# Convolution groups side by side: new places for the stages of entering chunks in rounds two and three

## The chip, the cores and the metric

The kernel runs on one core of one Trainium2 chip. The metric is the device time of one launch in microseconds (us), lower is better. Engines are named as the profile names them: PE (TensorE matmul), PEld (TensorE weight load), DVE (VectorE), ACT (ScalarE), POOL (GpSimd) and SP (SyncE, which only issues DMAs here).

## The reference

Eight batches of 4224 tokens with 192 channels pass through a causal convolution and then through a mixing block. Biases and norms are absent; this is all of it:

```python
w = softmax(weight, axis=-1)            # 8 heads x 7 taps
x = causal_conv(x, w)                   # 7 taps per head of 24 channels
theta = x @ w_theta                     # (192, 192)
zr, zi = x * cos(theta), x * sin(theta)
y = w_tok_r @ zr + w_tok_i @ zi         # two (4224, 4224) token matrices
u = x + y
out = u + maximum(u @ w_ch, 0.0)        # (192, 192)
```

The two token matrices carry nearly all of the arithmetic.

## The kernel before

**Tiles.** The 4224 tokens are cut into 33 input chunks of 128 tokens (`NK`) and 33 output blocks of 128 rows (`NT`). A chunk's tile `z` holds seven half-width products of `x`, cosine and sine (`Z11`, `T1`, `Z21`, `Z22`, `T2`, `T4`, `T3`). A fast matrix product with seven instead of eight block products works on *pairs* of output blocks. So one **step** (class `Step`) takes one pair of output blocks and all active chunks, and consists of seven **runs** (`runs`), one for each block product: for each active chunk two matmuls 128x384 at L443 (the "y" matmuls). Where only one output block is left the step has four runs. Between the runs a result is added into the SBUF tile `pv` by DVE (`give`, L408). The PSUM pool of the accumulators (`ypool`) has two buffers. Three accumulators `c1`, `c2` and `c3` use them in one step; `c3` opens in run six, in the buffer that `c2` left after run four, and the next step's `c1` opens in the buffer that `c3` left.

**Rounds.** At most eleven chunks are active (`NW`). There are 58 steps, numbered t = 0 to 57 here, and three rounds of chunks: 0 to 10, 11 to 21 and 22 to 32. A chunk stays for 17 steps (`NU`). `start` tells at which step it becomes active. Chunks of rounds two and three become active at steps 18 to 23 and 36 to 41, two at a time, but one alone (15 and 26) at steps 20 and 38. They are prepared one step earlier, in steps 17 to 22 and 35 to 40, between the y matmuls of the nine chunks that are active there (ten in steps 19 and 37). Step 40 has only four runs. The first round is prepared by a loop of its own at the end of the kernel.

**The stages of a chunk** (class `Chunk`, `tasks`) are nine: `conv(0)`, `conv(1)`, `transpose`, `theta(0)`, `theta(1)`, the two `product`s and the two `sums`. `conv(j)` is a *convolution group*: eight small matmuls 96x192 on 64 columns at L210 into a PSUM tile `pc`, which ACT copies into `z` (L151); after `conv(1)` SP writes the convolved rows to `xs` in DRAM (L227, four DMAs). `transpose` is twelve PE transposes (L165) and an ACT copy to `uT` (L151). `theta(g)` is eight matmuls (L141) and two ACT sines into `z` (L246). `product` (L251) and `sums` (L257) are DVE work. The PSUM tiles of `conv`, `transpose` and `theta` share one pool of two buffers (`mmpool`).

**Order.** The orders of PE, DVE and ACT are written out by hand: `in_order` ties each instruction to the one before it on its engine. `mix` yields the y matmuls, and at its places calls *events*: pairs of a place and a function, sorted by place. A place runs from 0 to 7 over the whole step, whatever its number of runs, and an event comes ahead of the first chunk whose place is not smaller than its own:

```python
while events and events[0][0] * len(runs) <= 7 * (r + c / self.n):
    events.pop(0)[1]()
```

`step_events(t)` gathers the events of step t: the weight work of step t+1 (`w_tasks`: `turn` at L336 turns a staged weight tile, `wsum` at L348 makes sums of them), the loads of the `pv` tiles of step t+1 at place 1.6 (`load_rows`, L372), the loads of the token matrices of step t+2 at 1.3 and 4.3 (`load_w`, L323, into two `st` buffers), the loads of the chunks that are prepared in step t+1 at 4.5 (`load_chunk`: four DMAs of `x` from POOL at L197, and at L188 four of the 16 rows of history from the chunk before, from SP), and the nine stages of each chunk that becomes active at t+1. SP writes finished `pv` tiles to `part` at the end of a step (L456). SP's own queue and the `x` loads are not tied by hand; the framework places them.

Of the kernel before, what the change touches and what calls it, by code (L numbers as in the profile page):

```python
# [16 lines left out]
def kernel(  # L17
# [34 lines left out]
    NK = S // P  # L52
# [8 lines left out]
    NW = 11  # L61
# [4 lines left out]
    start = [base[k % NW] + (NU + 1) * (k // NW) for k in range(NK)]  # L66
# [20 lines left out]
    def dve(ins):  # L87
        return in_order("dve", ins)
# [4 lines left out]
    def pool(ins):  # L93
        return in_order("pool", ins)
# [31 lines left out]
    def channel_pieces(w):  # L126

        return ((slice(0, P), 0, w[0:P, :]), (slice(0, R), 1, w[P:D, :]),
                (slice(R, P), 2, w[0:R, :]), (slice(0, P), 3, w[R:D, :]))
# [145 lines left out]
    def load_chunk(k):  # L275
        if k < NK and k not in chunks:
            chunks[k] = Chunk(k, before=chunks[k - 1] if k % NW else None)
# [235 lines left out]
    def step_events(t):  # L513
        found = []
        s = steps[t]
        if t + 1 < NSTEP:
            found += steps[t + 1].w_tasks()
            found.append((1.6, steps[t + 1].load_rows))
            for i in steps[t + 1].adds:
                found.append((2 + 2 * i, lambda i=i: steps[t + 1].load_x(i)))  # L520
                found.append((3.6 + 2 * i, lambda i=i: steps[t + 1].add_x(i)))
        here = [(r, i, which) for r in steps for i, when, which in r.ahead if when == t]
        for j, (r, i, which) in enumerate(here):
            found.append((1.5 + 1.8 * j, lambda r=r, i=i, which=which: r.add_ahead(i, which)))
        if t + 2 < NSTEP:
            nxt = steps[t + 2]
            for m in (1, 2):
                found.append((1.3 + 3 * (m - 1), lambda m=m: nxt.load_w(m)))
        if t == NU - 2:
            def load_wch():  # L530
                dve(nc.vector.memset(wch[:, 1:3, :], 0.0))
                for rows, i, part_w in channel_pieces(moe_w_ch):
                    pool(nc.gpsimd.dma_start(out=wch[rows, i, :], in_=part_w))
            found.append((3, load_wch))
        for at, f in outputs:
            begin = at - sum(s.time for s in steps[:t])
            if 0 <= begin < steps[t].time:
                found.append((7 * begin / steps[t].time, f))
        if t >= NU - 2:
            new = [k for k in range(NK) if start[k] == t + 2 and k >= NW]  # L540
            for k in new:
                found.append((4.5, lambda k=k: load_chunk(k)))
            at = 0.1
            for k in (k for k in range(NK) if start[k] == t + 1 and k >= NW):
                pos = [0, .5, 1.4, 2.2, 2.6, 3.1, 3.15, 3.4, 3.6]

                def add(at, j, k):
                    def go():
                        if j == 0:
                            chunks[k].todo = chunks[k].tasks()  # L550
                        next(chunks[k].todo)()
                    found.append((at, go))
                for j, p in enumerate(pos):
                    add(at + p, j, k)
                at += 2.3
        return found


# [62 lines left out]
    for q in range(Q):  # L621
# [3 lines left out]
            start=True, stop=True,  # L625
# [11 lines left out]
    def stream():  # L637
        for t in range(NSTEP):
            yield from steps[t].mix(step_events(t))
# [104 lines left out]
```

## Time and profile before

| | us |
|---|---|
| three runs | 1448.31, 1449.44, 1449.76 |
| median | 1449.44 |
| span of the profiled execution, its own time | 1444.6 |
| PE busy | 1414.5 (98%) |
| DVE busy | 978.2 (68%) |
| POOL busy, ACT busy | 434.6 (30%), 316.2 (22%) |

The span runs from the first to the last instruction of the one execution that was profiled. Nothing around it is recorded for that execution; the three runs lie 3.7 to 5.2 us above it. The mean granted TensorE clock was 0.997. "Busy" of PE is the union of matmuls whose ends are modelled, so it does not say how fast they follow each other. The window 380 to 580 holds the entering steps of round two, 840 to 1030 those of round three.

### The profile page before, as it was taken

The page shows a single profiled execution, that of the slowest core. Times are in us where ns is not written, and L with a number is a line of the kernel's source. Part 1 is how long each engine was busy: PE and PEld are TensorE (multiplying, and loading weights), DVE is VectorE, ACT ScalarE, POOL GpSimd, SP SyncE. Part 2 cuts the span into 40 slices and gives each one's busy share as a digit, 9 for nine tenths or more (in the row PEclk, how much of TensorE's full clock was granted, in tenths as well). Part 3 has the DMA queues.
Part 4 walks back from the last instruction along what each step waited for, and adds up shares of the span by engine and source line. Part 5 has one row for each costly group of instructions (what it writes and reads, how often), then busy time and mean ns, then how long its engine had stood idle before and what let it go on. Part 6 is the DMA issues. An engine that isn't in the chain of part 4 may idle for free.

```text
span 1444.6 us, 23749 instructions
## 1 busy us (share of the span) xinstructions
PE 1414.5 (98%) x9809; PEld 886.3 (61%) x9809; DVE 978.2 (68%) x1050; ACT 316.2 (22%) x379; POOL 434.6 (30%) x655
## 2 busy tenths in 40 slices
PE   7899999999999999999999999999999999999997
PEld 4656666666666666666666666666666666666665
DVE  6893554555448687866666657876877677767686
ACT  6851101111124254000000004435210110010133
POOL 8421211111223232432433343233323123213120
PEclk9999999999999999999999999999999999999999
DMA  9975756564699999897899889989999999898883
GB/s 181 253 148 136 146 119 133 98 152 87 152 229 210 226 244 222 219 265 173 223 245 222 233 155 239 235 181 237 274 220 202 213 204 221 204 200 193 166 232 116
DMA packets 272029, 281.99 MB, mean 195 GB/s; under 512 B 106672, under 2 KB 240176, under 8 KB 271920
## 3 DMA queue, kind: packets, MB, share of 16 engines
q0 software_dynamic: 162464, 92.15, 48.4%
q1 hardware_dynamic: 71824, 178.88, 35.2%
q10 hardware_dynamic: 37632, 9.44, 4.3%
q8 instruction: 77, 1.26, 0.4%
q14 instruction: 32, 0.26, 0.1%
HBM read 245.49 MB, written 108.13 MB: 245 GB/s over the span
## 4 chain that ended last, share of the span: by engine, by line
PE 89%; DVE 3%; DMA 2%; ACT 2%; POOL 1%; issue 1%; SPq 0%; DVEq 0%; ACTq 0%; POOLq 0%
PE y L443 81%; PE v L141 5%; PE pc L210 1%; PE tp L165 1%; ACT z L246 1%; DVE pv L408 1%; DMA xw<-xw 1%; POOL xw L197 1%; DMA xw<-in_x_dram 1%; DVE z L257 1%; POOL st L323 1%; DVE z L251 1%; DMA pv<-part 1%; ACT uT L151 1%; DVE wt L336 0%
## 5 line engine op out<-in xcount | busy, mean ns | idle before, releaser
L443 PE MATMUL y<-z,wt 128*128 128x384 f16 x7656 | 1283.6, 326 | 10.4 <-DVE pv L408 7.3
L443 PEld LDWEIGHTS <-wt 128*128 128x128 f16 x7656 | 740.7, 98 | 488.1 <-issue 10.2
L408 DVE TENSOR_TENSOR pv<-y,pv 128x768 f32<-128x768 f32 x324 | 309.2, 955 | 327.0 <-PE y L443 286.8
L336 DVE STREAM_TRANSPOSE wt<-st 128x1408 f16<-128x1408 f16 (+7 forms) x224 | 327.8, 1465 | 45.8 <-PE y L443 39.1
L323 POOL DMA_DIRECT2D st<-in_moe_w_tok_r_dram x232 | 132.4, 579 | 464.9 <-DVE wt L336 459.4
L323 POOL DMA_DIRECT2D st<-in_moe_w_tok_i_dram x232 | 132.5, 580 | 405.4 <-DVE wt L336 397.5
L348 DVE TENSOR_TENSOR wt<-wt 128x1408 f16<-128x1408 f16 (+7 forms) x216 | 176.1, 815 | 40.5 <-PE y L443 38.0
L151 ACT ACTIVATE z<-pc 128x768 f16<-128x768 f32 x65 | 53.3, 820 | 386.7 <-PE pc L210 386.5
L151 ACT ACTIVATE ub<-pv 128x768 f16<-128x768 f32 x63 | 50.2, 835 | 333.2 <-DVE pv L408 310.7
L406 ACT ACTIVATE pv<-y 128x768 f32<-128x768 f32 x66 | 54.0, 819 | 281.6 <-PE y L443 281.6
L141 PEld LDWEIGHTS <-uT 128*128 128x128 f16 x1056 | 91.1, 98 | 27.4 <-issue 8.5
L386 POOL TENSOR_TENSOR pv<-pv,xr 128x1536 f32<-128x1536 f32 x24 | 74.5, 3105 | 67.1 <-DVE pv L476 21.9
L197 POOL DMA_DIRECT2D xw<-in_x_dram x132 | 76.5, 591 | 30.1 <-DMA xw<-xw 9.7
L476 DVE SCALAR_TENSOR_TENSOR pv<-v,pv 128x768 f32<-128x768 f32 x66 | 62.9, 954 | 27.5 <-PE v L141 27.0
L151 ACT ACTIVATE uT<-tp 128x1536 f16<-128x1536 f16 (+1 forms) x49 | 59.7, 1221 | 74.4 <-PE tp L165 74.4
L257 DVE TENSOR_TENSOR z<-z 128x768 f16<-128x768 f16 x132 | 73.4, 556 | 3.6
L246 ACT ACTIVATE z<-v,half_pi 128x768 f16<-128x768 f32 x66 | 59.9, 907 | 42.1 <-PE v L141 41.7
L251 DVE TENSOR_TENSOR z<-z 128x1536 f16<-128x1536 f16 x66 | 60.1, 948 | 6.6 <-ACT z L246 6.6
L141 PE MATMUL v<-wth,uT 128*128 128x192 f16 x528 | 55.0, 248 | 5.6 <-ACT z L246 3.3
L141 PE MATMUL v<-wch,uT 128*128 128x192 f16 x528 | 54.2, 246 | 2.1 <-DVE pv L476 1.2
L246 ACT ACTIVATE z<-v 128x768 f16<-128x768 f32 x66 | 53.5, 810 | 0.0
L210 PE MATMUL pc<-xw,bands 96*64 96x192 f16 x528 | 35.3, 256 | 1.2 <-DVE bands L628 0.8
(43 smaller groups left out, 138.0 us busy)
## 6 DMA issues: line engine op xcount, KB each, us to landing
part<-pv SPq DMA_DIRECT2D x79, 768.0 KB, 4.6
pv<-part SPq DMA_DIRECT2D x79, 768.0 KB, 6.0
out_dram<-pv SPq DMA_DIRECT2D x66, 384.0 KB, 4.3
st<-in_moe_w_tok_r_dram POOLq DMA_DIRECT2D x136, 176.0 KB, 5.7
st<-in_moe_w_tok_i_dram POOLq DMA_DIRECT2D x136, 176.0 KB, 5.1
xs<-z SPq DMA_DIRECT2D x132, 96.0 KB, 4.1
xw<-in_x_dram POOLq DMA_DIRECT2D x121, 96.0 KB, 5.9
xr<-xs SPq DMA_DIRECT2D x24, 384.0 KB, 4.5
```

The source lines that it names most:

```text
L141: pe(nc.tensor.matmul(v[:, k, b * D : (b + 1) * D], lhsT=tT[:, 3 * k + b + i, :], rhs=w[:, 2 * b + i, :], start=(i == 0), stop=(i == 1),))
L151: act(nc.scalar.activation(out=out, in_=in_, func=AT.Copy))
L197: nc.gpsimd.dma_start(out=self.xw[lo : lo + n, h, :, :], in_=x[:, t0 : t0 + n, :].rearrange("b s d -> s b d"),)
L246: act(nc.scalar.activation(**args))
L251: dve(nc.vector.tensor_tensor(out=o, in0=xv, in1=o, op=ALU.mult))
L257: dve(nc.vector.tensor_tensor(out=z[:, o, :], in0=z[:, a, :], in1=z[:, b, :], op=ALU.subtract))
L323: pool(nc.gpsimd.dma_start(out=st[a * Q : (a + 1) * Q, 0:nb, :, 0:n] .rearrange("i r bt s -> i (r bt) s"), in_=w[self.tbs[0] * P : (self.t ...
L336: dve(nc.vector.transpose(self.w[name][:, 0 : self.n, :, :], self.st[int(name[1])][:, int(name[0]) - 1, :, 0 : self.n * Q] .rearrange("p b ...
L348: dve(nc.vector.tensor_tensor(out=self.w[name][:, 0 : self.n, :, :], in0=self.w[a][:, 0 : self.n, :, :], in1=self.w[b][:, 0 : self.n, :, : ...
L386: ins = pool(nc.gpsimd.tensor_tensor(out=self.pv[i], in0=self.pv[i], in1=self.xr[i], op=ALU.add))
L408: dve(nc.vector.tensor_tensor(out=o, in0=yv, in1=o, op=ALU.add))
L443: pe(nc.tensor.matmul(y[cn][:, q, 0:BH], lhsT=self.w[wn][:, c, :, :].rearrange("p bt i -> p (bt i)"), rhs=chunks[k].z[:, zn, q * BH : (q + ...
```

## The change

Before, the second chunk of a step simply followed 2.3 places behind the first, with `conv(0)` and `conv(1)` half a place apart and the first chunk's stages at 0.1 plus the list `pos`. Now each of the two chunks has its own list of places, and both convolution groups of a chunk have the same place.

```diff
-            at = 0.1
-            for k in (k for k in range(NK) if start[k] == t + 1 and k >= NW):
-                pos = [0, .5, 1.4, 2.2, 2.6, 3.1, 3.15, 3.4, 3.6]
+            places = (
+                (.1, .1, 1.1, 2.75, 3.05, 3.6, 3.65, 3.9, 4.1),
+                (2.1, 2.1, 3.55, 4.6, 5.0, 5.5, 5.55, 5.8, 6.0),
+            )
+            new = [k for k in range(NK) if start[k] == t + 1 and k >= NW]
+            for k, pos in zip(new, places):
...
                 for j, p in enumerate(pos):
-                    add(at + p, j, k)
-                at += 2.3
+                    add(p, j, k)
```

The order of the nine numbers is that of the nine stages. In absolute places the list of the first chunk was 0.1, 0.6, 1.5, 2.3, 2.7, 3.2, 3.25, 3.5, 3.7, and that of the second chunk 2.4, 2.9, 3.8, 4.6, 5.0, 5.5, 5.55, 5.8, 6.0. No instruction is added or taken away.

## The prediction

> **What bounds the kernel now.** I read the page's busy times first (PE 98%), then the chain that ended last in order of time, since a busy PE does not say that it is fast.
>
> ```profile
> 102.48 315.10 PE y L443 x1938
> ...
> 571.62 295.75 PE y L443 x1820
> ```
>
> Outside the entering steps the chain is nothing but y matmuls: 315.10 / 1938 = 0.1626 us each. Steps without entering chunks can neither gain nor lose. Inside the entering steps I read PE's timeline, and, at the kernel's start, the one place where two convolution groups already stand together:
>
> ```profile
> 417.51 0.52 PE L210 MATMUL pc<-xw,bands 96*64 96x192 f16 x8
> 417.96 1.80 PE L443 MATMUL y<-z,wt 128*128 128x384 f16 x10
> 419.69 0.52 PE L210 MATMUL pc<-xw,bands 96*64 96x192 f16 x8
> ```
>
> ```profile
> 8.89 1.49 PE L210 MATMUL pc<-xw,bands 96*64 96x192 f16 x16 [0.78 <-DVE bands L628]
> ```
>
> From one group's start to the next, 419.69 - 417.51 = 2.18 us pass with ten y matmuls between (1.63): a lone group costs 0.55 us. Within a group the matmuls run in pairs (two halves of 64 columns). Sixteen in a row at the start last 1.49 us at about half clock; without the last matmul's 0.37 that is 1.12 over seven intervals, 0.16 a pair, so 0.08 at full clock, and no hole where the second group begins. Four pairs are 0.32 to 0.35 us. So going from y to convolution and back costs 0.20 to 0.23 us that a group standing behind another does not pay.
>
> Then the waits of PE: in the windows 380 to 580 and 840 to 1030 there are few, so stalls are no large pot. The longest is in the two steps with ten chunks, at 490.76 and 940.56; the chain around the first:
>
> ```profile
> 483.57 0.96 DVE pv L408
> 484.53 0.67 DVE wt L348
> 485.19 1.74 DVE z L251 x2
> 486.93 0.67 DVE wt L348
> 487.60 0.48 DVE z L257
> ...
> 489.84 0.88 DVE pv L408
> 490.72 0.04 issue
> 490.76 1.30 PE y L443 x7
> ```
>
> DVE gives run three, then S1, both products, S2 and all four sums, and only then the result of run four. `c3` waits for that buffer at the start of run six.
>
> **The change part by part.** Twelve steps (17 to 22, 35 to 40) prepare 22 chunks. The order of the built program confirms that all 22 have sixteen convolution matmuls in a row.
>
> *Adjacent groups.* I take 0.22 us a chunk (ends 0.20 and 0.23; bounded below by nothing, if the second group had to wait for its PSUM buffer: it uses the other of the two, long free, and the row at 8.89 shows no hole). Twenty chunks outside step 40: -4.4 us. [...]
>
> *Ten-chunk steps (19, 37).* S2 now stands ahead of the products and two of the four sums behind run four's give. From give three's start, by the rows of the chain: 0.9 + 0.67 + 0.67 + 1.74 + two sums 1.1 = 5.1, then the give 0.9: 6.0 us, where it was 7.2; and give three starts about 0.9 earlier (one theta of 0.66 and 0.22 no longer ahead of it). PE needs the buffer at run six, twenty chunk slots of 0.325 plus a theta behind run three's end, 7.2 us. The 0.73 us wait goes; with its ramp the y matmuls lose 0.9 each time. -1.8 us.
>
> *Nine-chunk steps, DVE.* At 429.73 to 445.3 DVE runs without idle time: it is nearly a second bound. Between gives three and six the same instructions lie (13.6 us by their starts, 429.73 to 443.37). Give three comes 0.65 us earlier, but products wait for theta(1)'s sine (ready 2.0 after give three's start; DVE gets there at 2.2, so no loss), and give four waits 0.3 for run four's end. So DVE ends 0.3 earlier while PE arrives 0.44 earlier; the next step's `c1` had 0.4 us to spare and keeps about 0.25. Where the weights of the next step are for ten chunks (steps 18 and 36; turns 1.50 for 1.37) that is overdrawn by about 0.15 each: +0.3 us, between 0 and 1.
>
> *ACT and PSUM buffers.* Two copies of 0.81 now follow each other; the second is done some 2.5 us into the step, the transposes come at 4.1. Transposes to theta: 18 or 20 y matmuls (2.9 us) cover the copy of 1.45. The sines of theta(0) (1.7) are over before the second transposes (2.9 after theta's end). Nothing is late; without this cover each chunk would lose up to 1.5.
>
> *Step 40.* Four runs, so places are dense. DVE is full to the last give at 1023.05 to 1024.0, which PE awaits at 1024.06. Before its products it stood idle 1.32 us for a sine; now S2 (0.88) fills that, while the sine comes about 0.15 later. PE resumes 0.7 earlier: -0.7, its two chunks' 0.44 included; theta(0)'s wait for `uT` remains (0.3 to 0.6) but is hidden behind this give.
>
> *SP and POOL.* The `xs` writes and the histories of the next chunks are issued 1 to 4 us earlier. In steps 17, 20, 35, 38 and 39 the first `pv` load stood ahead of the first `xs` writes, and now both `pv` loads stand behind them (some 3 us later for the first). They are needed a step later, so nothing waits, but they then move beside the `x` loads.
>
> *The second chunk's data.* This is the cost. Its first group comes 22 - 19 = 3 slots (0.97), a theta (0.66) and 0.22 earlier: 1.85 us, at 7.7 us into the step instead of 9.55. Its `x` is the last load that POOL issues in the step before, behind the token matrix, which waits for DVE's turn, and it shares the DMA engines with `part` (768 KB twice). Asked for the L197 loads at 890 to 893 and 441 to 444:
>
> ```profile
> L197 POOL DMA_DIRECT2D xw<-in_x_dram x4: 586/598/603, 890.5 to 892.2; - x4
> ...
> DMA to landing us min/median/max: 6.0/7.2/10.8
> ```
>
> ```profile
> L197 POOL DMA_DIRECT2D xw<-in_x_dram x4: 581/583/583, 441.9 to 443.6; - x4
> ...
> DMA to landing us min/median/max: 3.6/5.7/5.9
> ```
>
> Chunk 25's last load lands at 892.2 + 10.8 = 903.0, and its convolution starts at 903.26: 0.2 us to spare. Chunk 19's lands at 522.6 + 9.8 = 532.4 for 533.63: 1.2 to spare. Chunk 14's has 4.1, chunk 30's 5.9, the others more. POOL's issue keeps its distance to the step's end. With 1.85 less to spare, PE waits 1.65 for chunk 25 and 0.65 for chunk 19: 2.3 us. Ends: nothing, if all land like 14; 6.6, if 14, 19, 25 and 30, whose loads stand alike, all land like 25. I take 2.9, above the plain 2.3 since the `pv` loads now crowd such steps.
>
> Sum: -4.4 - 1.8 + 0.3 - 0.7 + 2.9 = -3.7 us. It is made against the span of 1444.6, so 1440.9; the later steps are PE's chain up to 1369, and carry it whole. The median lies 4.8 above that span: 1445.7.
>
> **Rivals.** *Late x decides* (the slower side): one mechanism, the wait of the second chunk's convolution for its `x`. Seven chunks (14, 17, 19, 21, 25, 28, 30) have loads issued at the end of a step; each that lands like 25's costs 1.65. The gains of 6.6 are gone with four late, and with six the kernel is 3.3 slower, with all seven 5 slower: 1454.4. For: 2 of 7 already land that late, and DMA queues are at 0.9 to 1.4 busy there. Against: 17, 21, 28 and 30 land 3 to 5 us into the step. Chance 0.14. *Four late*: the gain just gone, 1449.4, chance 0.16. *No late x*: earlier histories and `xs` writes leave the engines freer at the step's end; all terms but the last, -6.6: 1442.8, chance 0.17. *Adjacency gives nothing*: the switch is paid again between the groups; -1.8 - 0.7 + 0.3 + 2.9 = +0.7: 1450.1, chance 0.08; the row at 8.89 speaks against it. The forecast, with one to three late: 0.45.
>
> **How the numbers follow.** 0.2% is 2.9 us, about what a measurement of this kernel can tell from no change: faster means below 1446.5, slower above 1452.3. Two thirds of the forecast (1444 to 1447.5), all of no late x, and a part of four late: 0.51 faster. Slower is the late-x rival: 0.14. The rest, 0.35, is within. The range goes from a little under no late x (0.23 a group, 1442.3) to adjacency without gain (1450.2).
>
> **What would show it.** Right: sixteen-matmul convolution pieces of about 0.85 us; a two-chunk step 0.4 shorter than 26.68 (417.51 to 444.19); no wait at the start of run six in the ten-chunk steps; waits of PE for DMA `xw` at the second chunk of steps 21 and 36. Wrong: a hole inside the sixteen; y waiting for DVE at every step's start, which would say that DVE had become the bound; late `x` in five chunks or more.

## The result and the profile after

| | before | after |
|---|---|---|
| median of five runs beside each other, us | 1449.44 | 1441.24 |
| lowest to highest | 1447.99 to 1450.35 | 1440.74 to 1445.68 |
| span of the profiled execution | 1444.6 | 1439.4 |
| PE busy, DVE busy | 1414.5, 978.2 | 1410.6, 977.7 |

The changed kernel's time is 0.9956 of the time before, with an interval of 0.9945 to 0.9967: 4.8 to 8.0 us faster, 6.4 in the middle. The two medians lie further apart, 8.2. The profiled execution of after took 1441.24, 1.84 more than its span.

The chain that ended last, kernel after (start, us, what; the two long y stretches that the prediction showed, and the first after step 40):

```profile
103.77 315.10 PE y L443 x1938
...
569.61 295.75 PE y L443 x1820
...
1019.13 33.96 PE y L443 x208
```

The stretches last to the hundredth what they lasted before (315.10 and 295.75), so nothing changed between the rounds. Their starts, less those before (102.48, 571.62, 1024.06), say where the time went: +1.29, -2.01, -4.93. The kernel's start was 1.29 longer, round two saved 3.30 and round three 2.92, in all 6.2. The start is the same instructions in both. In the fourteen profiles of this study (the experiments' too) the first y matmul of step 7 came at anything from 166.3 to 169.7 us, so the +1.29 is within chance, and it is why the spans differ by 5.2 only.

PE's timeline, kernel after (start, us, line, operation, count):

```profile
418.80 0.85 PE L210 MATMUL pc<-xw,bands 96*64 96x192 f16 x16
...
423.19 3.09 PE L443 MATMUL y<-z,wt 128*128 128x384 f16 x18
426.20 0.85 PE L210 MATMUL pc<-xw,bands 96*64 96x192 f16 x16
426.99 2.12 PE L443 MATMUL y<-z,wt 128*128 128x384 f16 x12
...
445.03 0.85 PE L210 MATMUL pc<-xw,bands 96*64 96x192 f16 x16
```

The sixteen are one piece of 0.85. From 423.19 to 426.99 are 3.80 us; eighteen y matmuls take 2.93 of them, so two adjacent groups cost 0.87 where two lone ones cost 2 x 0.55. From the starts of the y matmuls on both sides it is 0.877 against 1.094, 0.217 less, for every one of the 22 chunks but the one whose data came late. The two-chunk step from 418.80 to 445.03 lasts 26.23, 0.45 less than 26.68.

PE's waits between 380 and 1030 us, kernel after (who waited for whom: us in total, times, longest):

```profile
PE y L443 <- DVE pv L408: 1.4, 1, 1.4
PE pc L210 <- DMA xw<-in_x_dram: 0.3, 1, 0.3
PE v L141 <- ACT uT L151: 0.3, 1, 0.3
```

Before, y waited there for DVE three times (1.8 in total), among them the two waits of the ten-chunk steps at 490.76 and 940.56. Both are gone; the one left is at the start of step 41. (`v` is the PSUM tile of `theta`.) PE's timeline shows it, and also the one convolution whose `x` came late, that of chunk 28:

```profile
950.92 0.27 PE L210 MATMUL pc<-xw,bands 96*64 96x192 f16 x1
951.47 0.85 PE L210 MATMUL pc<-xw,bands 96*64 96x192 f16 x15 [0.28 <-DMA xw<-in_x_dram]
...
1019.13 2.11 PE L443 MATMUL y<-z,wt 128*128 128x384 f16 x12 [1.39 <-DVE pv L408]
```

The profile's idle time goes by modelled ends of matmuls. A *hole* below goes by starts: the distance between two neighbouring y matmuls less the usual 0.163 us. For the last row that is 1.55.

### The profile page after: what moved, and what is told of

It is laid out like the page before. It is cut to its first block, busy times and chain, and to the rows that moved or that the text cites. A ratio compares the mean times of both kernels' runs of the same rounds, so it can differ in the third digit from the quotient of the medians.

```text
span 1439.4 us, 23742 instructions
## 1 busy us (share of the span) xinstructions
PE 1410.6 (98%) x9809; PEld 890.2 (62%) x9809; DVE 977.7 (68%) x1050; ACT 316.0 (22%) x379; POOL 435.2 (30%) x655
## 4 chain that ended last, share of the span: by engine, by line
PE 89%; DVE 4%; DMA 2%; ACT 2%; issue 1%; POOL 1%; DVEq 0%; SPq 0%; ACTq 0%
PE y L443 81%; PE v L141 5%; PE tp L165 1%; DMA xw<-in_x_dram 1%; PE pc L210 1%; ACT z L246 1%; DMA xw<-xw 1%; DVE pv L408 1%; DVE z L257 1%; DVE z L251 1%; DVE wt L336 1%; POOL st L323 0%; DVE pv L476 0%; ACT uT L151 0%; DVE wt L348 0%
## 5 line engine op out<-in xcount | busy, mean ns | idle before, releaser
L197 POOL DMA_DIRECT2D xw<-in_x_dram x132 | 76.3, 585 | 28.2 <-DMA xw<-xw 8.3
L210 PE MATMUL pc<-xw,bands 96*64 96x192 f16 x528 | 31.4, 255 | 1.4 <-DVE bands L630 0.8
```

What stands on the lines that cost most here:

```text
L197: nc.gpsimd.dma_start(out=self.xw[lo : lo + n, h, :, :], in_=x[:, t0 : t0 + n, :].rearrange("b s d -> s b d"),)
```

## The experiments

All kernels made for the experiments share one substitution, so they are compared with each other. The 24 transposes of output blocks in steps 41 to 52, which ran as DMA transposes, run as PE transposes with an ACT copy. This costs some 15 us behind round three (base 1463.45 us, the kernel before on the same chip 1448.44) and leaves the steps before 41 as they are:

```diff
-            crossed(self.uT[i], self.ub[i])
+            transposed(self.uT[i], self.ub[i], range(NG))
...
-                    found.append((at + 2, lambda i=i: self.cross_u(i)))
+                    found.append((at + 4, lambda i=i: self.cross_u(i)))
```

Ratios are to the kernel before, run on the same chip. The first four kernels of the table ran on one chip, the next four on another, then two and two. Across these groups the intervals, some 2 us to each side, do not tell kernels apart that differ by one or two us; there the stages decide. "Stages" are three stretches of the profiled execution, between the first y matmuls of steps 17 and 23, 35 and 41, 41 and 43: round two, round three, and what follows the last entering step. The steps from 7 to 17 and from 23 to 35 took 250.25 and 289.57 in nearly every kernel.

| kernel | median us | ratio, interval | stages us |
|---|---|---|---|
| base | 1463.45 | 1.0102, 1.0088 to 1.0115 | 160.22, 153.15, 54.51 |
| changed | 1456.95 | 1.0059, 1.0046 to 1.0071 | 156.92, 148.83, 55.58 |
| spacing_alone | 1461.88 | 1.0101, 1.0086 to 1.0116 | 159.41, 151.41, 55.57 |
| adjacent_alone | 1471.74 | 1.0155, 1.014 to 1.0171 | 164.65, 156.55, 55.06 |
| dve_order_alone | 1462.28 | 1.0096, 1.008 to 1.0113 | 159.46, 152.34, 54.51 |
| x_loads_ahead | 1457.96 | 1.0066, 1.0053 to 1.0078 | 156.92, 148.58, 58.02 |
| sums_later | 1459.22 | 1.0073, 1.0057 to 1.009 | 157.02, 149.72, 54.27 |
| sums_later_x_ahead | 1455.96 | 1.005, 1.0036 to 1.0063 | 157.84, 148.44, 54.74 |
| sums_later_x_ahead_but_last | 1455.96 | 1.0039, 1.0025 to 1.0052 | 156.92, 148.58, 54.27 |
| changed_again | 1457.79 | 1.0055, 1.0043 to 1.0068 | 156.92, 149.33, 55.58 |
| base_without_histories | 1463.3 | 1.0103, 1.0088 to 1.0118 | 160.22, 153.11, 54.51 |
| changed_without_histories | 1457.28 | 1.0059, 1.0042 to 1.0076 | 156.92, 148.58, 55.82 |

The theory: the gain is the switch between y and convolution, paid once for each chunk instead of twice, with a smaller part from DVE's new order. The rival: the new spacing makes the gain, and adjacency adds nothing.

### The frame: base and changed

The kernel before and the changed kernel, both with the substitution and nothing else.

> The kernel before with one substitution that all experiments share: the 24 transposes of output blocks in steps 41 to 52, which ACT gives to the DMA engines, are done by PE and copied by ACT, as the kernel does for entering chunks. Steps 17 to 40 are those of before. Twelve transposes cost PE 0.67 us between y matmuls: 24 x 0.67 = 16 us more, 1465.5. All other experiments are read against this one. For the late data: if chunks 19 and 25 land some 9 us into their step because of the old order, they do it here again; if that is chance, other chunks do.

> The changed kernel with the same substitution. All theories: faster than the base by what the change gave, 6.4 us in the timed runs (interval 4.8 to 8). Theory (switching plus buffers): in its profile, from the end of round one's long chain of y to the start of the next, 3.2 us less in round two (11 x 0.217, 0.9 for the ten-chunk step, 0.1 back) and about 3 less in round three; waits for x at most once. Rival (late x by chance): other chunks wait, 1 to 3 us in sum.

The medians differ by 6.5 us, where the original pair's ratio gives 6.4. The stages give it again: -3.30, -4.32 and +1.07. So the substitution left the change's effect as it was.

### The new places without adjacency: spacing_alone

```diff
-                (.1, .1, 1.1, 2.75, 3.05, 3.6, 3.65, 3.9, 4.1),
-                (2.1, 2.1, 3.55, 4.6, 5.0, 5.5, 5.55, 5.8, 6.0),
+                (.1, .6, 1.1, 2.75, 3.05, 3.6, 3.65, 3.9, 4.1),
+                (2.1, 2.6, 3.55, 4.6, 5.0, 5.5, 5.55, 5.8, 6.0),
```

> The new places, with conv(1) half a place behind conv(0) again (0.6 and 2.6). Theory (switching plus buffers): the switch of 0.217 us comes back 22 times, 4.8 us, and what the spacing does by itself stays: the 0.9 us wait of the two ten-chunk steps is gone, step 40 gains some tenths. About 2 faster than the base, and 4.4 to 4.8 slower than the changed kernel. Rival (the order of DVE and the spacing make the gain): within 1 us of the changed kernel, 6 faster than the base. Late x: the second chunk's conv(0) still asks 1.6 us earlier than in the base, so if the late data matter they show here too, as waits of PE for DMA xw.

Its median is 1.6 below base, which the times cannot tell apart (runs up to 1466.5); the stages give 1.5. It is 4.9 above `changed`, all runs above all of `changed`. In round two `changed` is 2.49 shorter, which is 0.226 for each of eleven chunks; in round three 2.58. This is adjacency by itself, at the size of the theory, and the rival falls.

### Adjacency in the old places: adjacent_alone

```diff
-            at = 0.1
...
-                pos = [0, .5, 1.4, 2.2, 2.6, 3.1, 3.15, 3.4, 3.6]
+            places = (
+                (.1, .1, 1.5, 2.3, 2.7, 3.2, 3.25, 3.5, 3.7),
+                (2.4, 2.4, 3.8, 4.6, 5.0, 5.5, 5.55, 5.8, 6.0),
```

> The base's places, with conv(1) moved to the place of conv(0) in both chunks and nothing else. Theory (switching plus buffers): the switch is saved 22 times, 4.8 us, but in the ten two-chunk steps the second chunk's conv(1) now takes the PSUM buffer that theta(0) of the first chunk still holds until its two sines are done, 2.5 us after theta's start, where PE arrives after 1.3: a hole of about 1.1 us inside the sixteen matmuls, 10 times, 11 us. The ten-chunk wait of 0.9 stays. Sum: about 6 slower than the base, and the new spacing is what makes adjacency pay. Rival (adjacency alone does it, the spacing is idle): 4.8 faster than the base.

It is 8.3 slower than base, where about 6 was expected. PE's timeline and its waits between 380 and 1030 us:

```profile
428.06 0.82 PE L141 MATMUL v<-wth,uT 128*128 128x192 f16 x8
428.72 0.49 PE L443 MATMUL y<-z,wt 128*128 128x384 f16 x2
429.14 0.52 PE L210 MATMUL pc<-xw,bands 96*64 96x192 f16 x8
430.57 0.52 PE L210 MATMUL pc<-xw,bands 96*64 96x192 f16 x8 [0.91 <-ACT z L246]
```

```profile
PE pc L210 <- ACT z L246: 9.1, 10, 0.9
```

In the old places `theta(0)` of the first chunk (428.06) stands two y matmuls ahead of the second chunk's convolution. Its PSUM tile is one of the pool's two and is held until ACT's sines are done, so the second group finds no buffer: a hole of 0.9 in the middle of the sixteen, ten times in ten second chunks (1.1 each from start to start). Holes of y behind DVE at eight step starts, 0.28 to 1.04 us each, add some 3 us over base. So adjacency pays only together with a spacing in which both buffers are free, and the two parts of the change are not a sum.

### DVE's new order alone: dve_order_alone

The old places, but the first chunk's products and sums later, where the change has them:

```diff
-            at = 0.1
...
-                pos = [0, .5, 1.4, 2.2, 2.6, 3.1, 3.15, 3.4, 3.6]
+            places = (
+                (.1, .6, 1.5, 2.3, 2.7, 3.6, 3.65, 3.9, 4.1),
+                (2.4, 2.9, 3.8, 4.6, 5.0, 5.5, 5.55, 5.8, 6.0),
```

> All convolution, transpose and theta places as in the base; only the first chunk's products and sums at 3.6 to 4.1. Theory (switching plus buffers): S2 goes ahead of the products and sums go behind run four's result, so the two waits of 0.9 at the start of run six go, and step 40 resumes up to 0.7 earlier: about 2 faster than the base, 1461.5, the same as the new places with the groups apart. Rival (those waits went because theta moved, not because of DVE's order): no change, 1463.4. Loads of x stand as in the base, where chunk 25 landed last again: if the old order makes it late, it does here too.

Round two fell by 0.76 and round three by 0.81; the median fell by 1.2, which is within the intervals. Both waits of the ten-chunk steps are gone, so it is DVE's order that removes them. Each was worth 0.9 and two holes of 0.19 at the next steps' starts came in return. Step 40 did not become shorter (19.56 against 19.57): its gain needs the other new places as well.

### The x loads ahead of the token matrix: x_loads_ahead

`changed`, with POOL's `x` loads tied into its order and asked a little earlier, so that all four stand ahead of the token matrix:

```diff
+                if k >= NW:
+                    pool(ins)
...
-                found.append((4.5, lambda k=k: load_chunk(k)))
+                found.append((4.25, lambda k=k: load_chunk(k)))
```

> The changed kernel (with the experiments' substitution), and the x loads of entering chunks tied into POOL's order ahead of the second token matrix (place 4.25 for 4.5). Theory (the changed kernel loses only about 0.3 us to late x, at chunk 28): at most 0.5 is to be had, within 1 us of 1456.95; x lands several us before it is asked for in every chunk, and no wait of PE for DMA xw is left; the token matrix behind it has a step to spare. Rival (late x costs 2 to 3 us in the timed runs, other than in the one profiled): 1454 to 1455.

No convolution waits for `x` any more, yet the median is 1.0 above `changed`, within the intervals, and the three stages together are 2.2 longer. Waits of PE from 380 to 1030 us, then of DVE from 1000 to 1030 us (the two added lines move every number behind them by two):

```profile
PE y L445 <- DVE pv L410: 3.7, 2, 2.3
PE v L141 <- ACT uT L151: 0.3, 1, 0.3
```

```profile
DVE wt L338 <- DMA st<-in_moe_w_tok_r_dram: 3.5, 1, 3.5
```

The token matrix now stands behind the `x` loads. At the end of the four-run step DVE waits 3.5 us for it, PE stands behind DVE, and step 41 lasts 29.01 for 26.57. A wait of `x` was exchanged for a longer wait of the token matrix, at the one step where that has no time to spare.

### The second chunk's sums behind the last give: sums_later, sums_later_x_ahead

The 1.4 at 1019.13 comes from four sums (2.3 us) that DVE does just ahead of the give that PE awaits. Here they come behind it, first by themselves and then with the edit of `x_loads_ahead`:

```diff
-                (2.1, 2.1, 3.55, 4.6, 5.0, 5.5, 5.55, 5.8, 6.0),
+                (2.1, 2.1, 3.55, 4.6, 5.0, 5.5, 5.55) + ((6.05, 6.1) if s.pair else (6.9, 6.95)),
```

> The changed kernel (with the experiments' substitution), and the second chunk's sums behind the give that PE awaits: at 6.05 and 6.1, in step 40 at 6.9 and 6.95. Theory (what is left of stalls in the entering steps is DVE's order): the wait of 1.55 at the start of step 41's run two goes, and 0.14 at each of two step starts: 1.8 faster, 1455.1. Step 40's theta then still waits 0.45 for uT, now in the open. Rival (DVE as a whole is the bound of step 40): the wait only moves to the next give, and the time stays within 0.5 of 1456.95.

> Both additions to the changed kernel at once: x loads ahead of the second token matrix and the second chunk's sums behind the awaited give. Theory (switching plus buffers plus DVE's order): 1.8 for the sums and 0.3 for the data, 2.1 faster than the changed kernel, 1454.9; no wait of PE for DMA xw or for a give is left in rounds two and three. Rival (freed PE time only makes the x loads later relative to it, or DVE the bound): no more than 1 faster.

The first did in its profile what it should: the hole at step 41's start fell from 1.55 to 0.25 us, and the two small DVE holes went. But chunk 14's `x` was late by 0.25 us and chunk 25's by 1.3, as PE's timeline of `sums_later` shows for chunk 25:

```profile
897.17 0.27 PE L210 MATMUL pc<-xw,bands 96*64 96x192 f16 x1
898.46 0.85 PE L210 MATMUL pc<-xw,bands 96*64 96x192 f16 x15 [1.02 <-DMA xw<-in_x_dram]
```

Its six runs lie between 1454.7 and 1462.6, and their median is 2.3 above `changed`, though its profiled stages are 0.3 shorter. That the slower ones are slow through more late `x` is likely but not shown: only one of them was profiled, and it was the fastest. With the `x` loads ahead the spread shrinks to 1454.0 to 1456.9 and the median is 1.0 below `changed`, within the intervals. What remains there are holes of y behind DVE in round two, 0.66 us at 468.59 and 0.41 at 471.92. The later sums alone do not make them, since `sums_later` has the same sums and no such hole. The chain shows DVE held up just before, by a token matrix that now stands behind the `x` loads (start, us, what). It was on its way for 13.97 us, and DVE stood idle for the last 3.56 of them:

```profile
443.38 13.97 DMA st<-in_moe_w_tok_i_dram
457.48 1.51 DVE wt L338
```

### Only the last pair left as it was: sums_later_x_ahead_but_last, and changed once more

The tie and the earlier place for chunks up to 30 only, the second chunk's sums back at 5.8 and 6.0 in full steps:

```diff
+                if NW <= k < 31:
+                    pool(ins)
...
+                found.append((4.5 if k > 30 else 4.25, lambda k=k: load_chunk(k)))
...
+                (2.1, 2.1, 3.55, 4.6, 5.0, 5.5, 5.55) + ((5.8, 6.0) if s.pair else (6.9, 6.95)),
```

> Changed, with the x loads issued from place 4.25 ahead of the token matrix for chunks 14 to 30 (the last pair, 31 and 32, stays as in changed), and the second chunk's sums at 5.8 and 6.0 in full steps and 6.9 and 6.95 in the four-run step. Theory: with the x asked early no convolution waits for it; the token matrix of step 41 is no longer behind x loads, so the 2.4 us at 1023.24 of x_loads_ahead do not come; the sums after the last give of the four-run step take 1.3 of the 1.55 us away. So 1.5 to 2.5 us under changed, some 1455, and a y hole of at most 0.4 at the start of step 41. Rival (the wait for the token matrix comes from the earlier loads of chunks 29 and 30 as well): a y hole of over 1 us behind step 40 again, and no gain over changed.

> The changed order a second time, beside the other kernel of this call. If which chunk's x comes late is decided by the order alone, chunk 28 is the late one again, by 0.2 to 0.5; if chance decides, another chunk or none. Its time says how far two medians of one kernel lie apart: within 1 us by the ranges so far.

Of all PE's waits between 380 and 1030 us, this one is left in the first:

```profile
PE v L141 <- ACT uT L151: 0.3, 1, 0.3
```

Its hole at step 41's start is 0.24 us. Its three stages add up to 359.77, where `changed` has 361.33 and `changed_again` 361.83. The median is 1.8 below `changed_again` on the same chip, and each of its six runs lies below each of the five, though the intervals of the two ratios overlap: a gain of 1.5 to 2 us over the change. No wait of DVE for a token matrix is longer than 1.0 us there. `changed_again` lies 0.8 from `changed`, and chunk 28 is the late one again, by 0.7 us.

### No histories to load: base_without_histories, changed_without_histories

Every chunk takes its sixteen rows of history from DRAM with its own `x` load:

```diff
-                if before is not None:
+                if before is not None and k <= NW:
```

> The old places; for chunks 12 to 21 and 23 to 32 the sixteen rows of history come with the chunk's own x load from DRAM (48 rows for 32, half as many bytes more) and not from the chunk before, so SP issues none of the four history DMAs. In the old places chunk 25's last load took 10.8 and 11.05 us and chunk 19's 9.8 and 9.2, with the histories issued less than 1 us ahead of it or together with it. Theory (the histories, in flight with the token matrix, hold back the x behind them): both take 5 to 8.5 us now, so that over 2.5 us stay to spare for each. Rival (it is the part writes and the bytes that are on the way at the end of a step): 9 us or more for both. The time stays within 1 us of base by the first, a little above it by the second.

> The same with the new places. There the histories were already 1.8 to 2.5 us ahead of the second chunks' x, and chunk 28 was the late one three times out of three (9.8 to 10.3 us, a wait of 0.2 to 0.7). Theory: 19 and 25 stay at 5 to 8.5 us, and 28, whose histories went with its first x loads, comes earlier, under 9 us, with no wait of PE for x. Rival (part writes and bytes): 28 takes 10 us or more, 14, 19 and 25 come later too, and PE waits 0.5 us or more; the time is 0.5 to 3 us above changed.

In the old places the last loads of 25 and 19 took 5.2 and 5.7 us for 11.05 and 9.2, and in the new places 28's took 8.85, with no wait of PE for `x`. These are the theory's numbers. Against it, two other last loads became longer in the new places: chunk 17's 9.73 for 7.59 in `changed`, chunk 32's 9.23 for 4.82; each load now brings half as many rows more. And the framework also placed the `x` loads anew: only two of chunk 25's four stood behind the token matrix in the old places, one in the new ones. So the histories and the place in POOL's queue are not separated. The times stayed where they were.

## Why the prediction was right, and where not

| step of the sum | predicted us | measured us |
|---|---|---|
| adjacent groups, twenty chunks | -4.4 | -4.3 |
| waits of the ten-chunk steps | -1.8 | -1.8 |
| DVE at the nine-chunk steps | +0.3 | +0.2 |
| step 40 with its two chunks, and its give | -0.7 | -0.6 |
| late `x` of second chunks | +2.9 | +0.5 |
| sum | -3.7 | -6.0 |

The measured terms come from the y matmuls of the two profiled executions; the stages themselves give -6.2.

**Where it came out.** The median of 1441.24 lies 1.1 below the low end of the stated range, 1442.3; by the ratio the change takes 1449.44 to 1443.1, which is inside. (0.23 us a chunk instead of 0.22, which is said to give that low end, gives 1442.6.) The outcome stands nearest to the rival *No late x*, at -6.6 and with a chance of 0.17. One chunk was late, as the forecast's condition says, but another one than those named, and for 0.5 us instead of 1.65.

**Adjacency** is 0.217 a chunk for the 0.22 that was read from two rows of before (the clock granted in the row at 8.89 was 0.50, in that at 417.51 1.00), and `spacing_alone` against `changed` gives 4.9 us by the clock and 5.1 by the stages. Where in a group it stands can be seen in PE's timeline of before, which has a convolution group and a `theta` between y matmuls:

```profile
414.81 2.76 PE L443 MATMUL y<-z,wt 128*128 128x384 f16 x16
417.51 0.52 PE L210 MATMUL pc<-xw,bands 96*64 96x192 f16 x8
...
423.42 2.44 PE L443 MATMUL y<-z,wt 128*128 128x384 f16 x14
425.70 0.82 PE L141 MATMUL v<-wth,uT 128*128 128x192 f16 x8
426.36 0.49 PE L443 MATMUL y<-z,wt 128*128 128x384 f16 x2
```

Sixteen y matmuls take 2.60 of the 2.70 us up to the convolution: 0.09 to 0.10 is paid on entering. The starts of single matmuls show as much again on leaving (0.178 where 0.079 lies between pairs) and 0.025 between the first two pairs. Fourteen take all of the 2.28 us up to `theta`, whose eight matmuls lie 0.0825 apart and fill the 0.66 up to the next y: this group, with weights of the stream's own size, 128x128, pays nothing beyond its matmuls. So here the price goes with the 96x64 weights; whether with their rows or their columns, and why, stays open. The lower bound given, a second group that must wait for its PSUM buffer, is real: it is what `adjacent_alone` shows, 0.9 us at each of ten second chunks.

**The ten-chunk waits** went as reasoned, through the order on DVE. **At the nine-chunk steps** the holes came at the two places named, 0.148 at 470.99 and 0.145 at 917.47, where before had 0.06 each. **Step 40** and the next went from 45.08 to 44.47. Here the total was right and the picture was not: PE does not resume after a shorter wait. It reaches the give 1.7 earlier and waits about 1.1 longer, because DVE is the chain there, with both products and the four sums ahead of the give. The chain of after, start, us and what:

```profile
1014.10 1.75 DVE z L251 x2
...
1018.13 0.96 DVE pv L408
1019.09 0.04 issue
1019.13 6.01 PE y L443 x36
```

**Late x** is the mis-sized term. Its first half held: the last load of chunk 25 is issued 8.96 us ahead of the convolution for 11.04, that of 19 8.94: 2.1 us nearer, for the 1.85 reckoned. What failed is the second half, that a chunk's loads would take as long as before. Chunk 25's took 7.0 for 10.8 and 19's 4.9 for 9.8. Both came in time, 2.0 and 4.0 us early, so the waits of PE named for the second chunks of steps 21 and 36 did not appear. `changed` and `changed_again`, the same order, took 8.2 and 6.1 for 25 and 8.1 and 4.8 for 19: shorter than in before and base each time, but with as little as 0.75 us to spare. Chunk 28, which had 6.25 to spare before, was the late one: its last load is issued 2.8 nearer to the convolution (9.59 us for 12.39) and takes 10.1 for 6.1. The `x` issues at L197, kernel after, for chunk 25 (888 to 890.5 us) and the last two of chunk 28 (940 to 942 us):

```profile
L197 POOL DMA_DIRECT2D xw<-in_x_dram x4: 578/578/578, 888.3 to 890.0; - x4
...
DMA to landing us min/median/max: 4.9/5.0/7.0
```

```profile
L197 POOL DMA_DIRECT2D xw<-in_x_dram x2: 578/578/578, 940.8 to 941.3; - x2
...
  PE pc L210: 0.3, 1
...
DMA to landing us min/median/max: 7.8/9.0/10.1
```

For these two chunks, what else was issued beside the last load goes with its length, over the nine kernels that leave both the history loads and the request at 4.5 as they are:

| chunk, what was issued beside | last load to landing, us |
|---|---|
| 25, histories' last issue 0.9 us ahead of the first `x`, or with it (before, base) | 10.8, 11.05 |
| 25, 1.8 to 3.3 us ahead, `part` write 1 us behind the last `x` (after and five others) | 5.2 to 8.2 |
| 25, 2.3 us ahead, but `part` write 0.13 ahead of the last `x` (sums_later) | 10.2 |
| 28, `part` write 0.3 to 0.6 behind the last `x` (before and three others) | 5.7 to 8.1 |
| 28, `part` write 0.2 to 0.3 ahead (after and four others) | 8.2 to 10.3 |

In the new places the histories of 25 are some 1.3 us further ahead of its `x`, and for chunk 28 two loads instead of one stand behind the token matrix, so that the last is issued behind `part`. Of the other second chunks, 19 agrees on the histories: 9.2 to 9.8 us with their last issue under 1 us ahead of its first `x` or with it (before, base, `dve_order_alone`), 4.8 to 8.1 in the six others. But chunk 21 took 5.7, 5.3 and 5.4 us with histories 0.9, 1.0 and 0.6 us ahead (before, base, `dve_order_alone`). And with a `part` write just ahead of the last `x`, by 0.05 to 0.15 us, chunk 19 took 7.1 in `sums_later` and chunk 14 took 5.7 to 7.4 in eight kernels. So neither neighbour is enough by itself, and that they cause the lengths of 25 and 28 is a reading of nine traces. The experiments without histories agree with it for 19, 25 and 28 and not for 17 and 32, and they moved the loads as well, so the cause of the lengths stays open. What late `x` can cost is shown by `sums_later`, 1.3 us for one chunk; no profile here had more than two such chunks.

**From span to median** the prediction added 4.8, the distance of the median from one span. In the profiled executions of after and of the experiments, whose own times are known, only 1.8 to 2.2 us lie outside the span, so that execution of before took about 1446.6, an estimate. The other 2.8 say that it was a quick one: its step 7 began at 166.84, near the low end of what the same instructions did in all profiles. Of the 4.5 between 1445.7 and 1441.24, late `x` makes 2.4, this offset 3.0 and the smaller terms 0.4; the 1.3 of the start goes against them.

## What to carry to other kernels

Where a small matmul group of another shape interrupts a long stream, its cost can have a fixed part for the switch (here 0.22 of 0.55 us), to be read as group start to group start less the stream's own matmuls. Put groups together, but first see that the PSUM buffers of all of them are free there, else the saved 0.2 becomes a hole of 0.9. A spare time of a load, measured in one order, was no constant here: when the order moved, the load's length moved too (chunk 25, 10.8 us before and 7.0 after), and even one order gave lengths 3 us apart (chunk 19, 4.8 to 8.1), so read it from more than one profile. And compare spans between profiles only behind the kernel's start, which alone varied by 3.4 us here, from one named instruction to another.

## What the runs showed of the hardware that was not expected

- The last 96 KB load of a second chunk's `x` took from 4.3 to 11.05 us from issue to landing in the nine kernels of the table above. With its issue 2.1 us nearer to its use, chunks 19 and 25 landed further ahead of their use in after than in before, by 2.8 and 1.7 us; between base and `changed` it was 0.8 further for 25 and 1.0 less for 19.
- Switching from the stream's matmuls, with weights 128x128, to the convolution's, with weights 96x64, and back costs PE 0.217 us at a granted clock of 1.00 beyond the matmuls themselves, the same within 0.003 us for all of after's chunks but the one whose data came late. `theta`, with weights 128x128, pays no such price: its eight matmuls fill 0.66 us, 0.0825 each.
- The start of the kernel, up to step 7, varied by 3.4 us between profiles (166.3 to 169.7) with the same instructions, while the two long stretches of y, 315.10 and 295.75 us, were the same in before and after.
